# Attention and SoLU feed-forward on one core: u turned by block DMAs and VectorE's block transposes instead of by TensorE

## Chip, cores, metric

One core of one Trainium2 chip, all data in float32 (the two weights arrive as 64-bit floats and are taken apart by the kernel). The metric is the device time of one execution in microseconds (us), the median of several runs.

## The reference, cut to what matters

```python
# attention: batch 8, heads 8, 576 positions, head size 64
scores = scale * (q @ k^T)                       # 576 x 576 for each of 64 heads
scores = where(scores >= max - tau, scores, -1e9)
attn = exp(scores - max);  attn = attn / (sum + 1e-9)
x = (attn @ v)  -> (4608 tokens, 512)            # heads side by side

# feed-forward
h = x @ w_in                                     # 512 -> 1024
e = exp(h - max(h));  solu = h * e / (sum(e) + 1e-9)
ln = (solu - mean) / sqrt(var + 1e-6) * g_ln     # over the 1024
out = ln @ w_out                                 # 1024 -> 512
```

In the kernel `u` is h * e, before all scaling. A token tile has 128 tokens; there are 36.

## The kernel before

The kernel goes in 144 rounds. A round makes the scores of 128 query rows for two heads, and their threshold softmax; beside this, TensorE gets one more piece of work from a list: half of h, half of o (the product with w_out), or the attention with v of an earlier round. In the long middle four rounds repeat, and carry one token tile: h0, h1 (halves of h, with an attention each), o0, o1 (halves of o, of the tile before).

What each engine does, in the program's order (cut):

```python
# scores(s): s_ps, two tiles, ONE buffer each (4 PSUM banks)
nc.vector.tensor_reduce(out=nm, in_=ps[:, 0:S], axis=AX.X, op=ALU.max, negate=True)   # "maxima"
nc.scalar.activation(out=w, in_=ps[:, 0:S], func=AF.Prelu, bias=nth, ...)             # frees s_ps
nc.scalar.activation(out=w, in_=w, func=AF.Exp, ...)
nc.gpsimd.tensor_scalar(out=w, in0=w, scalar1=sm[:, x : x + 1], ...)                  # normalise
# blocks(s): 32x32 block transposes, then eight transfers put the blocks in place
nc.vector.transpose(out=T[:, :, r, h, :], in_=w)
nc.sync.dma_start(out=to[32 * a : ...], in_=T[...])           # wT <- T, x8 every second round
# attend: v times wT into a "pv" tile; next round ScalarE copies it out
nc.scalar.copy(out=to, in_=y)                                 # "attended", frees the pair of banks
```

PSUM is the memory that the matrix products are written to, in banks. `pv`, `h_ps` and `o_ps` share four more banks as two tiles of two banks (`take` hands out a free pair).

```python
def ff_exp(t):  nc.scalar.activation(out=d["u"], in_=d["h"], func=AF.Exp, ..., accum_out=d["se"])
def ff_mul(t):  nc.vector.tensor_tensor(out=d["u"], in0=d["h"], in1=d["u"], op=ALU.mult)

def u_item(t, f):                       # one half of u turned, rides on a round's scores
    def make(spare, x):
        for c in range(4):
            turn(spare, x + c, ...)     # 4 matmuls 64x64 with the identity into spare s_ps columns
    def keep(spare, x, r):
        (nc.vector.tensor_copy if r else nc.scalar.copy)(out=d["uT"][...], in_=seen(spare, r, x, 4))

def ff_o(t, part, split):               # one half of o: 32 matmuls 64x64 by 256
    for c in range(NC):
        for r in range(2):
            z = part ^ r                # row half r writes bank z; the banks change over at half time
            for y in range(2):
                mm = nc.tensor.matmul(out=o[ROWS[y], 512 * z : 512 * z + 256],
                    lhsT=d["uT"][ROWS[r], c, ROWS[y]], rhs=w2[ROWS[r], c, 256 * z : 256 * z + 256], ...)
                if part and not last: sync(mm, d["fence"])
# w2 is w_out * g_ln, centred over its rows, so that the mean needs no subtraction;
# ff_out: ob = o * rs  (rs = 1/sqrt(...) per token)
```

Of the kernel before, what the change touches and what calls it, by code (L numbers as in the profile page):

```python
# [20 lines left out]
def kernel(  # L21
# [43 lines left out]
    small = ctx.enter_context(tc.tile_pool(name="small", bufs=6))  # L65
# [4 lines left out]
    w2 = const.tile([P, NC, DM], F32, name="w2")  # L70
# [110 lines left out]

    def piece(x):
        if x < 2 * NP:
            c, hf = divmod(x, 2)
            cols = slice(512 * hf, 512 * hf + 512)
            return w_in[P * c : P * c + P, cols], w1[:, c, cols], W_UNIT
        c = x - 2 * NP
        return w_out[P * c : P * c + P, :], w2[:, c], gs[:, c : c + 1]
# [4 lines left out]
    def weight_load(x):  # L193
# [3 lines left out]
        (nc.scalar if x < 3 else nc.sync).dma_start(out=raw, in_=piece(x)[0])  # L197
        raws[x] = dict(raw=raw)

    def weight_a(x):  # L200
        if not wide:
# [4 lines left out]
            work.tile([P, 512], I32, tag=t, bufs=n, name="em") for t, n in (("em", 2), ("m", 1))  # L206
# [39 lines left out]
    totals = []  # L246

    def add_up(c):
        if c == 1:
            totals.append(work.tile([P, DM], F32, tag="ob", name="total"))  # L250
        if c:
            total = totals[0]
            nc.vector.tensor_tensor(
                out=total, in0=total if c > 1 else w2[:, 0], in1=w2[:, c], op=ALU.add
            )

    def mean():
        total = totals[0]
        ones = work.tile([P, P], F32, tag="ob", name="ones")
        nc.gpsimd.memset(ones, 1.0 / DFF)  # L260
        tag, m = take("mean")
        nc.tensor.matmul(out=m[:, 0:DM], lhsT=ones, rhs=total, start=True, stop=True)
        nc.scalar.copy(out=total, in_=m[:, 0:DM])
        pairs_free.append(tag)

    def center():
        for c in range(NC):
            nc.vector.tensor_tensor(out=w2[:, c], in0=w2[:, c], in1=totals[0], op=ALU.subtract)  # L268
# [162 lines left out]
    def ramp(s, x):  # L431
# [6 lines left out]
        w = work.tile([P, S], F32, tag="w", bufs=5, name="w")  # L438
# [24 lines left out]
    def blocks(s):  # L463
# [13 lines left out]
        u["wT"] = wT = work.tile([P, 2, NK, 2, 2, 32], F32, tag="wT", bufs=3, name="wT")  # L477
# [37 lines left out]
    def attended(key):  # L515
# [3 lines left out]
        if kind == 2:  # L519
            if b % 2 == 0:  # L520
                xe[b // 2] = work.tile([P, NP, P], F32, tag="xe", name="xe")
# [68 lines left out]
    def ff_stats(t):  # L590
# [18 lines left out]
        d["rs"] = rs  # L609


    def u_item(t, f):
        d = ffn[t]
        if f == 0:
            d["uT"] = work.tile([P, NC, P], F32, tag="uT", bufs=1, name="uT")
        d["turned"] = f + 1

        def make(spare, x):
            for c in range(4):
                o = P * (4 * f + c)  # L620
                turn(spare, x + c, lambda r, y: d["u"][ROWS[r], o + 64 * y : o + 64 * y + 64])

        def keep(spare, x, r):
            (nc.vector.tensor_copy if r else nc.scalar.copy)(
                out=d["uT"][:, 4 * f : 4 * f + 4, ROWS[r]], in_=seen(spare, r, x, 4)
            )

        return 4, make, keep


    def ff_t(t, f):
        d = ffn[t]
        if f == 0:
            d["uT"] = work.tile([P, NC, P], F32, tag="uT", bufs=1, name="uT")
        tp = ps_mm.tile([P, 1024], F32, tag="s1", name="tp_u")
        for c in range(4):
            o = P * (4 * f + c)
            nc.tensor.transpose(  # L638
                out=tp[:, P * c : P * c + P], in_=d["u"][:, o : o + P], identity=ident
            )  # L640
        (nc.vector.tensor_copy if f else nc.scalar.copy)(  # L641
            out=d["uT"][:, 4 * f : 4 * f + 4],
# [4 lines left out]
    def ff_o(t, part, split):  # L647
# [27 lines left out]
        if part == 0:  # L675
            d["fence"] = fence(last[-4:])
# [227 lines left out]
```

## Time and profile before

| | time | TensorE busy | VectorE | ScalarE | GpSimd |
|---|---|---|---|---|---|
| before | 963.9 us (962.7 to 966.0) | 93% | 66% | 68% | 49% |

The prediction below shows the lines. How to read them: a group has the source line, the engine, out<-in, the count, busy us, mean ns of one, and the idle time of that engine ahead of it with what ended it. In the windows view the columns are the stretch, its length, then busy us of TensorE (PE), its weight loads (PEld), VectorE (DVE), ScalarE (ACT), GpSimd (POOL), then the granted clock of TensorE, the DMA engines' share, and GB/s.

### The profile page before, as it was taken

Reading aid. Unit: us, or ns where it says so; the run is one execution under the profiler, and the core shown is the slowest. Engines: PE = TensorE matmul, PEld = TensorE weight load, DVE = VectorE, ACT = ScalarE, POOL = GpSimd, SP = SyncE. Lnnn points to the kernel's source line nnn. Section 1 sums busy time; section 2 is a strip of 40 time slices with the busy share of each in tenths; the row PEclk is TensorE's granted clock in tenths of the full one; section 3 lists DMA queues with packets and bytes.
Section 4 is the critical chain, followed back from the end, with each engine's and each line's share of the span. In section 5 each row is a group of like instructions: output and inputs, shape, how many; then the busy total and the mean of one; then the engine's idle time right before and its main releaser. Section 6 shows DMA issues by size and latency. Waiting matters only on the chain. (4 is left out here: it accounts for less than half of the span.)

```text
span 965.3 us, 43052 instructions
## 1 busy us (share of the span) xinstructions
PE 894.9 (93%) x18583; PEld 646.9 (67%) x18583; DVE 639.9 (66%) x1013; ACT 652.1 (68%) x1560; POOL 473.7 (49%) x898
## 2 busy tenths in 40 slices
PE   4657679999999999999999999999999999999997
PEld 3444446777767787777877776777867778665543
DVE  4889876667766667666666666666666666676221
ACT  5857656777867777777777776777777777776111
POOL 2886753555444545445454544445444555554111
PEclk9969798999999999999999999999999999999999
DMA  9897744875678447874678456864668445744200
GB/s 234 203 235 207 163 111 115 206 163 128 169 157 199 113 112 175 210 161 109 168 160 198 114 122 154 207 160 111 171 151 210 107 115 124 166 116 112 61 22 22
DMA packets 87037, 143.31 MB, mean 148 GB/s; under 512 B 28984, under 2 KB 61760, under 8 KB 86848
## 3 DMA queue, kind: packets, MB, share of 16 engines
q1 hardware_dynamic: 85616, 138.60, 60.4%
q8 instruction: 146, 2.39, 1.1%
q10 hardware_dynamic: 1232, 1.97, 0.7%
q14 instruction: 43, 0.35, 0.1%
HBM read 46.14 MB, written 9.44 MB: 58 GB/s over the span
## 5 line engine op out<-in xcount | busy, mean ns | idle before, releaser
L424 DVE TENSOR_REDUCE nm<-s_ps 128x1 f32<-128x576 f32 x288 | 204.7, 752 | 224.5 <-PE s_ps L408 224.4
L667 PE MATMUL o_ps<-w,uT 64*64 64x256 f32 x3968 | 233.7, 379 | 1.1 <-DVE w L268 1.1
L667 PEld LDWEIGHTS o_ps<-w,uT 64*64 64x64 f32 x3968 | 195.4, 134 | 51.9 <-issue 16.3
L439 ACT ACTIVATE w<-s_ps,nth 128x576 f32<-128x576 f32 x288 | 213.5, 741 | 22.2 <-issue 0.4
L459 POOL TENSOR_SCALAR w<-w,sm 128x576 f32<-128x576 f32 x288 | 215.4, 761 | 14.4
L449 ACT ACTIVATE w<-w,ntau 128x576 f32<-128x576 f32 x288 | 219.1, 764 | 0.0
L471 DVE STREAM_TRANSPOSE T<-w 128x576 f32<-128x576 f32 x288 | 207.8, 757 | 13.6 <-POOL w L459 6.6
L562 PE MATMUL h_ps<-w,xh 64*64 64x512 f32 x1856 | 214.7, 590 | 0.0
L435 ACT ACTIVATE nth<-nm,tau_t 128x1 f32<-128x1 f32 x288 | 85.9, 298 | 170.3 <-DVE nm L424 170.2
L510 PEld LDWEIGHTS pv<-wT,v 64*64 64x64 f32 x5760 | 166.0, 137 | 43.8 <-issue 39.4
L408 PE MATMUL s_ps<-kT,qT 64*64 64x512 f32 (+1 forms) x2048 | 171.9, 428 | 17.3 <-ACT w L439 12.4
L510 PE MATMUL pv<-wT,v 64*64 64x128 f32 (+1 forms) x5760 | 167.8, 264 | 12.2 <-DMA wT<-T 7.8
L456 POOL TENSOR_SCALAR sm<-sm 128x2 f32<-128x2 f32 x144 | 37.3, 259 | 277.8 <-ACT w L449 274.3
L562 PEld LDWEIGHTS h_ps<-w,xh 64*64 64x64 f32 x1856 | 107.5, 133 | 93.0 <-issue 88.0
L457 POOL TENSOR_TENSOR sm<-sm,mone 128x2 f32<-128x2 f32 x144 | 103.1, 716 | 12.0
L408 PEld LDWEIGHTS s_ps<-kT,qT 64*64 64x64 f32 x2048 | 57.3, 141 | 25.6 <-ACT w L439 19.0
L575 DVE TENSOR_REDUCE hm<-h_ps 128x1 f32<-128x1024 f32 x36 | 44.0, 1223 | 29.8 <-PE h_ps L553 18.0
L581 ACT ACTIVATE u<-h_ps,hm 128x1024 f32<-128x1024 f32 x36 | 40.1, 1114 | 28.4 <-DVE hm L575 27.7
L281 PE MATMUL s_ps<-ident,u 64*64 64x64 f32 x2016 | 50.0, 222 | 5.8 <-ACT w L439 2.4
L281 PEld LDWEIGHTS s_ps<-ident,u 64*64 64x64 f32 x2016 | 46.9, 135 | 12.3 <-ACT w L439 4.3
L449 ACT ACTIVATION_READ_ACCUMULATOR w<-w,ntau 128x1 f32 x288 | 54.7, 190 | 0.0
L104 POOL MEMSET mark<- 128x1 f32 x63 | 6.3, 99 | 95.8 <-PE o_ps L667 91.3
(89 smaller groups left out, 769.1 us busy)
## 6 DMA issues: line engine op xcount, KB each, us to landing
wT<-T SPq DMA_DIRECT2D x576, 144.0 KB, 3.2
v<-in_v_dram SPq DMA_DIRECT2D x64, 256.0 KB, 5.8
out_dram<-ob SPq DMA_DIRECT2D x32, 256.0 KB, 3.7
q<-in_q_dram SPq DMA_DIRECT2D x15, 512.0 KB, 5.7
k<-in_k_dram SPq DMA_DIRECT2D x15, 512.0 KB, 6.8
raw<-in_moe_w_out_dram SPq DMA_DIRECT2D x8, 512.0 KB, 5.4
raw<-in_moe_w_in_dram SPq DMA_DIRECT2D x5, 512.0 KB, 6.2
v<-in_v_dram SPq DMA_DIRECT2D x32, 64.0 KB, 5.5
```

Of the source, the lines that this page charges most:

```text
L281: nc.tensor.matmul(out=spare[r][ROWS[y], to], lhsT=lhsT_of(r, y), rhs=ident[ROWS[r], ROWS[r]], start=True, stop=True,)
L408: nc.tensor.matmul(out=ps[h][ROWS[y], ks], lhsT=lhsT, rhs=d["kT"][ROWS[h], ks], start=True, stop=True,)
L424: nc.vector.tensor_reduce(out=nm, in_=ps[:, 0:S], axis=AX.X, op=ALU.max, negate=True)
L435: nc.scalar.activation(out=nth, in_=d["nth"][x], func=AF.Identity, bias=tau_t, scale=1.0)
L439: nc.scalar.activation(out=w, in_=ps[:, 0:S], func=AF.Prelu, bias=nth, scale=1.0, alpha=1.0e30,)
L449: nc.scalar.activation(out=w, in_=w, func=AF.Exp, bias=ntau, scale=1.0, accum_out=sm[:, x : x + 1])
L457: nc.gpsimd.tensor_tensor(out=sm, in0=sm, in1=mone, op=ALU.pow)
L459: nc.gpsimd.tensor_scalar(out=w, in0=w, scalar1=sm[:, x : x + 1], scalar2=1.0, op0=ALU.mult, op1=ALU.mult)
L471: nc.vector.transpose(out=T[:, :, r, h, :], in_=w)
L510: nc.tensor.matmul(out=to, lhsT=d["v"][ROWS[u], h0 + h, m], rhs=rhs, start=m == 0, stop=m == NK - 1,)
L562: mm = nc.tensor.matmul(out=h[ROWS[y], f], lhsT=x[ROWS[r], c, ROWS[y]], rhs=w1[ROWS[r], c, f], start=part == 0 and c == 0, stop=part == 1 ...
L667: mm = nc.tensor.matmul(out=o[ROWS[y], 512 * z : 512 * z + 256], lhsT=d["uT"][ROWS[r], c, ROWS[y]], rhs=w2[ROWS[r], c, 256 * z : 256 * z + ...
```

## The change

The intent: take the turning of u (64 small matmuls with the identity per tile, and their evacuation) off TensorE, the engine that bounds the kernel. VectorE can transpose 32x32 blocks; to make a whole turn of those, eight transfers first move blocks of u across partitions into `V`. So that a row half of TensorE holds all features of its own tokens, w_out is kept twice (second copy with the row halves exchanged), and each row half adds up into one PSUM bank: no change of banks, no fence. u is normalised by ScalarE before it is moved, so w_out is not centred. For room, w has 4 buffers and not 5, wT 2 and not 3, small 3 and not 6, xe 1.

```diff
-    def u_item(t, f): ...                       # TensorE's turn, with its copies
+    def ff_norm(t):
+        nc.scalar.activation(out=d["u"], in_=d["u"], func=AF.Identity, bias=nb, scale=rs)
+    def ff_swap(t):
+        for r in range(2):
+            for g in range(2):
+                for y in range(2):
+                    to, of = 64 * r + 32 * g, 64 * r + 32 * y
+                    nc.sync.dma_start(out=V[to : to + 32, y],
+                        in_=d["u"][of : of + 32, DFF // 2 * g : DFF // 2 * g + DFF // 2])
+    def ff_turn(t, rnd):
+        nc.vector.transpose(out=uT, in_=d["V"].rearrange("p y (m x) -> p m y x", x=32))
     def ff_o(t, part):
+        for m in range(NC * part, NC * part + NC):
+            for r in range(2):
+                for z in range(2):
+                    nc.tensor.matmul(out=d["o"][ROWS[z], 512 * r : 512 * r + 256],
+                        lhsT=d["uT"][ROWS[r], m]..., rhs=w2[ROWS[r], m ^ r, 256 * z : 256 * z + 256], ...)
+    def weight_d(x):                            # the second copy of w_out
+        for r in range(2):
+            nc.sync.dma_start(out=w2[ROWS[r], 2 * c + 1], in_=w2[ROWS[1 - r], 2 * c])
-    add_up, mean, center                        # w_out's centring
 # schedule, rnd = the round h1 of the tile
-                middle.setdefault(rnd + 3, []).append(lambda t=cur: ff_stats(t))
+                middle.setdefault(rnd + 2, []).append(lambda t=cur: ff_stats(t))
+                late.setdefault(rnd + 2, []).append(lambda t=cur: (ff_norm(t), ff_swap(t)))
+                late.setdefault(rnd + 3, []).append(lambda t=cur, at=rnd + 3: ff_turn(t, at))
-                if busy and quarter < 2 and preps and ...: room = 0
+                if busy and quarter > 1 and preps and ...: room = 0
```

(Cut: w_out's loads in four 32-partition pieces, the order of g_ln, the output in two transfers, the buffers.)

More of the change, by code (lines that the diff above doesn't have):

```diff
@@ L64 @@
     work = ctx.enter_context(tc.tile_pool(name="work", bufs=2))
-    small = ctx.enter_context(tc.tile_pool(name="small", bufs=6))
+    small = ctx.enter_context(tc.tile_pool(name="small", bufs=3))
     ps_mm = ctx.enter_context(tc.tile_pool(name="ps_mm", bufs=1, space=PSUM))
@@ L69 @@
     w1 = const.tile([P, NP, DFF], F32, name="w1")
-    w2 = const.tile([P, NC, DM], F32, name="w2")
+    w2 = const.tile([P, 2 * NC, DM], F32, name="w2")
     mhalf = const.tile([P, 1], F32, name="mhalf")
@@ L179, in gains @@
         pairs_free.append(tag)
+    w_rows = w_out.rearrange("(g c r x) n -> c r g x n", g=2, r=2, x=32)
     def piece(x):
@@ L187, in piece @@
         c = x - 2 * NP
-        return w_out[P * c : P * c + P, :], w2[:, c], gs[:, c : c + 1]
+        return w_rows[c], w2[:, 2 * c], gs[:, c : c + 1]
     NW = 2 * NP + NC
@@ L196, in weight_load @@
         )
-        (nc.scalar if x < 3 else nc.sync).dma_start(out=raw, in_=piece(x)[0])
+        queue = nc.scalar if x < 3 else nc.sync
+        if x < 2 * NP:
+            queue.dma_start(out=raw, in_=piece(x)[0])
+        else:
+            for r in range(2):
+                for g in range(2):
+                    o = 64 * r + 32 * g
+                    queue.dma_start(out=raw[o : o + 32], in_=piece(x)[0][r, g])
         raws[x] = dict(raw=raw)
@@ L205, in weight_a @@
         d["em"] = e, m = [
-            work.tile([P, 512], I32, tag=t, bufs=n, name="em") for t, n in (("em", 2), ("m", 1))
+            work.tile([P, 512], I32, tag=t, bufs=n, name="em") for t, n in (("ob", 2), ("xe", 1))
         ]
@@ L243, in weight_c @@
         nc.gpsimd.tensor_tensor(out=dst, in0=dst, in1=d["em"][0].bitcast(F32), op=ALU.mult)
-    totals = []
-    def add_up(c):
-        if c == 1:
-            totals.append(work.tile([P, DM], F32, tag="ob", name="total"))
-        if c:
-            total = totals[0]
-            nc.vector.tensor_tensor(
-                out=total, in0=total if c > 1 else w2[:, 0], in1=w2[:, c], op=ALU.add
-            )
-    def mean():
-        total = totals[0]
-        ones = work.tile([P, P], F32, tag="ob", name="ones")
-        nc.gpsimd.memset(ones, 1.0 / DFF)
-        tag, m = take("mean")
-        nc.tensor.matmul(out=m[:, 0:DM], lhsT=ones, rhs=total, start=True, stop=True)
-        nc.scalar.copy(out=total, in_=m[:, 0:DM])
-        pairs_free.append(tag)
-    def center():
-        for c in range(NC):
-            nc.vector.tensor_tensor(out=w2[:, c], in0=w2[:, c], in1=totals[0], op=ALU.subtract)
+    def weight_d(x):
+        c = x - 2 * NP
+        if c >= 0:
+            for r in range(2):
+                nc.sync.dma_start(out=w2[ROWS[r], 2 * c + 1], in_=w2[ROWS[1 - r], 2 * c])
     SPARE = 7
@@ L437, in ramp @@
         )
-        w = work.tile([P, S], F32, tag="w", bufs=5, name="w")
+        w = work.tile([P, S], F32, tag="w", bufs=4, name="w")
         nc.scalar.activation(
@@ L476, in blocks @@
         T = T.rearrange("p (c m) r h x -> p c (m r h x)", c=2)
-        u["wT"] = wT = work.tile([P, 2, NK, 2, 2, 32], F32, tag="wT", bufs=3, name="wT")
+        u["wT"] = wT = work.tile([P, 2, NK, 2, 2, 32], F32, tag="wT", bufs=2, name="wT")
         to = wT.rearrange("p g m r h x -> p g (m r h x)")
@@ L520, in attended @@
             if b % 2 == 0:
-                xe[b // 2] = work.tile([P, NP, P], F32, tag="xe", name="xe")
+                xe[b // 2] = work.tile([P, NP, P], F32, tag="xe", bufs=1, name="xe")
             to = xe[b // 2][:, :, 64 * (b % 2) : 64 * (b % 2) + 64].rearrange(
@@ L608, in ff_stats @@
         nc.gpsimd.tensor_tensor(out=rs, in0=rs, in1=se, op=ALU.mult)
-        d["rs"] = rs
-    def u_item(t, f):
-        d = ffn[t]
-        if f == 0:
-            d["uT"] = work.tile([P, NC, P], F32, tag="uT", bufs=1, name="uT")
-        d["turned"] = f + 1
-        def make(spare, x):
-            for c in range(4):
-                o = P * (4 * f + c)
-                turn(spare, x + c, lambda r, y: d["u"][ROWS[r], o + 64 * y : o + 64 * y + 64])
-        def keep(spare, x, r):
-            (nc.vector.tensor_copy if r else nc.scalar.copy)(
-                out=d["uT"][:, 4 * f : 4 * f + 4, ROWS[r]], in_=seen(spare, r, x, 4)
-            )
-        return 4, make, keep
@@ L631, in ff_t @@
-    def ff_t(t, f):
-        d = ffn[t]
-        if f == 0:
-            d["uT"] = work.tile([P, NC, P], F32, tag="uT", bufs=1, name="uT")
-        tp = ps_mm.tile([P, 1024], F32, tag="s1", name="tp_u")
-        for c in range(4):
-            o = P * (4 * f + c)
-            nc.tensor.transpose(
-                out=tp[:, P * c : P * c + P], in_=d["u"][:, o : o + P], identity=ident
-            )
-        (nc.vector.tensor_copy if f else nc.scalar.copy)(
-            out=d["uT"][:, 4 * f : 4 * f + 4],
-            in_=tp[:, 0:512].rearrange("p (c q) -> p c q", c=4),
-        )
-        d["turned"] = f + 1
@@ L647, in ff_o @@
-    def ff_o(t, part, split):
+        nb = small.tile([P, 1], F32, tag="nb", name="nb")
+        nc.gpsimd.tensor_scalar(
+            out=nb, in0=mv[:, 0:1], scalar1=rs, scalar2=-1.0, op0=ALU.mult, op1=ALU.mult
+        )
+        d["norm"] = rs, nb
+    def ff_norm(t):
+        d = ffn[t]
+        rs, nb = d["norm"]
+        nc.scalar.activation(out=d["u"], in_=d["u"], func=AF.Identity, bias=nb, scale=rs)
+    def ff_swap(t):
+        d = ffn[t]
+        d["V"] = V = work.tile([P, 2, DFF // 2], F32, tag="V", bufs=1, name="V")
+        for r in range(2):
+            for g in range(2):
+                for y in range(2):
+                    to, of = 64 * r + 32 * g, 64 * r + 32 * y
+                    nc.sync.dma_start(
+                        out=V[to : to + 32, y],
+                        in_=d["u"][of : of + 32, DFF // 2 * g : DFF // 2 * g + DFF // 2],
+                    )
@@ L648, in ff_o @@
+    def ff_turn(t, rnd):
+        d = ffn[t]
+        d["uT"] = uT = work.tile([P, 2 * NC, 2, 32], F32, tag="uT", bufs=1, name="uT")
+        nc.vector.transpose(
+            out=uT, in_=d["V"].rearrange("p y (m x) -> p m y x", x=32)
+        )
+        d["turned"] = rnd + 1
+    def ff_o(t, part):
         d = ffn[t]
         if part == 0:
-            d["osplit"] = split
-            if split:
-                d["otag"], d["o"] = take("o_ps")
-            else:
-                d["o"] = ps_mm.tile([P, 1024], F32, tag="s0", name="o_ps")
@@ L655, in ff_o @@
-        o = d["o"]
-        if not d["osplit"]:
-            for c in range(4 * part, 4 * part + 4):
-                nc.tensor.matmul(
-                    out=o[:, 0:DM], lhsT=d["uT"][:, c], rhs=w2[:, c], start=c == 0, stop=c == NC - 1
-                )
-            return
-        last = []
-        for c in range(NC):
-            for r in range(2):
-                z = part ^ r
-                for y in range(2):
-                    mm = nc.tensor.matmul(
-                        out=o[ROWS[y], 512 * z : 512 * z + 256], lhsT=d["uT"][ROWS[r], c, ROWS[y]],
-                        rhs=w2[ROWS[r], c, 256 * z : 256 * z + 256],
-                        start=part == 0 and c == 0, stop=part == 1 and c == NC - 1,
-                    )
-                    if part and not last:
-                        sync(mm, d["fence"])
-                    last.append(mm)
@@ L675, in ff_o @@
-        if part == 0:
-            d["fence"] = fence(last[-4:])
+            d["otag"], d["o"] = take("o_ps")
+        for m in range(NC * part, NC * part + NC):
+            for r in range(2):
+                for z in range(2):
+                    nc.tensor.matmul(
+                        out=d["o"][ROWS[z], 512 * r : 512 * r + 256],
+                        lhsT=d["uT"][ROWS[r], m].rearrange("p y x -> p (y x)"),
+                        rhs=w2[ROWS[r], m ^ r, 256 * z : 256 * z + 256],
+                        start=m == 0, stop=m == 2 * NC - 1,
+                    )
@@ L680, in ff_out @@
         ob = work.tile([P, DM], F32, tag="ob", name="ob")
-        if d["osplit"]:
-            nc.scalar.activation(
-                out=ob.rearrange("p (z n) -> p z n", z=2),
-                in_=d["o"].rearrange("p (z n) -> p z n", z=2)[:, :, 0:256], func=AF.Copy,
-                scale=d["rs"],
-            )
-            pairs_free.append(d["otag"])
-        else:
-            nc.scalar.activation(out=ob, in_=d["o"][:, 0:DM], func=AF.Copy, scale=d["rs"])
         if len(t) == 1:
-            for x in range(2):
-                r = (2 * t[0] + x) * S + SM
-                nc.sync.dma_start(out=out[r : r + ST, :], in_=ob[ST * x : ST * x + ST])
+            rows = out.rearrange("(b s) m -> s b m", s=S)[SM:S, 2 * t[0] : 2 * t[0] + 2]
         else:
@@ L696, in ff_out @@
             rows = out[b * S : b * S + SM, :].rearrange("(p t) m -> t p m", t=4)
-            nc.sync.dma_start(out=rows[2 * kind + m], in_=ob)
+            rows = rows[2 * kind + m].rearrange("(r k) m -> k r m", r=2)
+        nc.scalar.copy(
+            out=ob.rearrange("p (r n) -> p r n", r=2),
+            in_=d["o"].rearrange("p (r n) -> p r n", r=2)[:, :, 0:256],
+        )
+        pairs_free.append(d["otag"])
+        for z in range(2):
+            nc.sync.dma_start(
+                out=rows[:, :, 256 * z : 256 * z + 256],
+                in_=ob[ROWS[z]].rearrange("p (r n) -> p r n", r=2),
+            )
     NS = len(slots)
@@ L741 @@
         load_v(0, 0)
-        nc.sync.dma_start(out=g_rows, in_=g_ln.rearrange("(c p) -> c p", p=P))
+        nc.sync.dma_start(
+            out=g_rows.rearrange("c (r g x) -> c r g x", r=2, g=2),
+            in_=g_ln.rearrange("(g c r x) -> c r g x", g=2, r=2, x=32),
+        )
         whole_pair(0)
@@ L754 @@
         quarter = 0
-        u_due = []
         w2_done = False
@@ L777 @@
                 room = SPARE
-                if u_due and u_due[0][0] <= rnd:
-                    _, t, f = u_due.pop(0)
-                    items.append(u_item(t, f))
-                    room -= 4
-                if busy and quarter < 2 and preps and rnd + 4 < first_slot(preps[0][3]):
+                if busy and quarter > 1 and preps and rnd + 4 < first_slot(preps[0][3]):
                     room = 0
@@ L794 @@
                 exps(rnd)
-            elif u_due and u_due[0][0] <= rnd:
-                for _, t, f in u_due:
-                    ff_t(t, f)
-                u_due = []
             if rnd in whole:
@@ L804 @@
                 weight_c(pieces[rnd - 1])
-            if pieces.get(rnd - 3) == 2 * NP + NC - 1:
-                mean()
             for job in middle.pop(rnd, []):
@@ L815 @@
             elif quarter == 2 or (prev is not None and not due):
-                if prev is None or (ffn[prev].get("turned") == 2 and w2_done):
+                if prev is None or (ffn[prev].get("turned", NS + rnd) <= rnd and w2_done):
                     step = ("o", 0)
@@ L829 @@
                 late.setdefault(rnd + 1, []).append(lambda t=cur: ff_mul(t))
-                middle.setdefault(rnd + 3, []).append(lambda t=cur: ff_stats(t))
+                middle.setdefault(rnd + 2, []).append(lambda t=cur: ff_stats(t))
+                late.setdefault(rnd + 2, []).append(lambda t=cur: (ff_norm(t), ff_swap(t)))
+                late.setdefault(rnd + 3, []).append(lambda t=cur, at=rnd + 3: ff_turn(t, at))
             elif step == ("o", 0):
                 if prev is not None:
-                    ff_o(prev, 0, rnd + 1 < NS)
+                    ff_o(prev, 0)
                 quarter = 3
@@ L836 @@
                 if prev is not None:
-                    ff_o(prev, 1, None)
+                    ff_o(prev, 1)
                     begin.setdefault(rnd + 1, []).append(lambda t=prev: ff_out(t))
-                if cur is not None:
-                    u_due += [(rnd + 1, cur, 0), (rnd + 2, cur, 1)]
                 prev, cur = cur, None
@@ L863 @@
                     weight_a(x + 1)
-            x = pieces.get(rnd - 2, -1) - 2 * NP
-            if x > 0:
-                add_up(x)
-            if pieces.get(rnd - 3) == 2 * NP + NC - 1:
-                center()
-                w2_done = True
+            if rnd - 2 in pieces:
+                weight_d(pieces[rnd - 2])
+                w2_done = pieces[rnd - 2] == NW - 1
             rnd += 1
```

## The prediction

> **What bounds the kernel now.** I read the page first, for busy shares and slices, then the windows by stage, then the timelines of TensorE, VectorE, ScalarE and the DMA queue around 340 to 360 us, then the timeline of the end.
>
> ```profile
> PE 894.9 (93%) x18583; PEld 646.9 (67%) x18583; DVE 639.9 (66%) x1013; ACT 652.1 (68%) x1560; POOL 473.7 (49%) x898
> PE   4657679999999999999999999999999999999997
> ...
> 164.50:891.00 726.50, 718.05 (x16114) 543.28 (x16107) 498.19 (x796) 534.28 (x1283) 362.99 (x727) 1.00 0.64 152
> 0.00:164.50 164.50, 110.88 (x2095) 71.49 (x2099) 122.92 (x194) 107.02 (x258) 102.28 (x147) 0.87 0.75 184
> 891.00:966.00 75.00, 65.99 (x381) 32.11 (x379) 18.80 (x25) 10.80 (x19) 8.39 (x24) 0.98 0.12 34
> ```
>
> From 164 to 891 us TensorE is busy 99% at the full clock, and nothing else is over 74%. So the long middle is TensorE's order of work; the start (weights, DMA) and the end (feed-forward of the last tiles) are stages of their own. The middle repeats every four rounds of scores: h first half, h second half, o first half, o second half (called h0, h1, o0, o1 here), one token tile a cycle. From the times at which ScalarE starts each round, the cycle is 23.9 us on average (round 20 at 150.5 us, round 142 at 879.1: 728.6 / 122 x 4).
>
> ```profile
> 353.21 3.72 PE L667 MATMUL o_ps<-w,uT 64*64 64x256 f32 x64
> 356.67 0.71 PE L281 MATMUL s_ps<-ident,u 64*64 64x64 f32 x30
> ...
> 355.27 1.51 DVE L471 STREAM_TRANSPOSE T<-w 128x576 f32<-128x576 f32 x2
> 358.36 1.42 DVE L424 TENSOR_REDUCE nm<-s_ps 128x1 f32<-128x576 f32 x2 [1.58 <-PE s_ps L408]
> ...
> 356.84 5.44 SPq L482 DMA_DIRECT2D wT<-T  x8
> ...
> wT<-T SPq DMA_DIRECT2D x576, 144.0 KB, 3.2
> SPq L482 <- DVE T L471: 318.0, 69, 9.5
> ```
>
> To see: one of the two transposes of u costs TensorE 0.5 us (356.67 until the scores start at 357.17). VectorE waits 1.6 us for scores, so it has slack, but only that. Eight transfers of one group keep the DMA queue for 5.4 us, 0.64 us from issue to issue; each lands 3.2 us after its issue (2.3 at the least). The queue spends 318 us waiting at its head for VectorE's T.
>
> **What the Trainium skill says.** "DMA: Bandwidth & Descriptors", section Rules for kernel authors: many small transfers should be made into a large one; below 64 KB one pays mostly overhead. The new ones have just 64 KB. The trace agrees in kind: 0.5 KB of tau took 4.3 us to land, 144 KB took 3.2. Same page, Anatomy of one DMA: DMA engines do not wait on semaphores; any wait is on the issuing sequencer before dispatch. The 318 us above are such waits, so whatever stands behind one in the queue waits too. "Perfetto Trace Analysis", Per-instruction lifecycle, on DMA: the reported time ends when the sequencer is free, the data movement comes after; hence 0.59 us in the timeline and 3.2 to land. "VectorE: DVE Perf Modes", The three transpose paths: VectorE transposes only 32x32 blocks; that is why DMAs must first move blocks across partitions.
>
> **The change, part by part.**
>
> Off TensorE: 36 tiles less the 4 or 5 of the end, two u-transposes each, 63 x 0.5 to 0.55 us = 33 us. The fences of o are worth under 3 us (TensorE's weight loads waited 2.6 us for the mark). The matrix products of o stay 64 per tile of 64x64 by 256, in four quadrants as before; I take 3.46 us a half as now (348.03 to 351.49). The preparations of q and k move from the o to the h rounds: no cost in sum.
>
> Off the evacuation: 63 copies on each of VectorE (414 ns) and ScalarE (364 ns). On: ScalarE one 128x1024 pass (as the exponential, 1.11 us), VectorE one 128x1024 transpose. T's 576 columns take 0.72 us, so 1024 take about 1.2. GpSimd one more small operation, 0.34. In sum ScalarE +17 us, VectorE +17 us: neither binds by its sum.
>
> On the DMA queue: eight 64 KB transfers a tile, 8 x 0.64 = 5.1 us, and one more output transfer. Two wT groups 10.9, V 5.1, outputs 1.3, loads (18 a batch of 4.5 tiles) 2.6: 20 of 23.9 us. It fits in sum. But the order counts. In the built program V's transfers stand directly behind a wT group, that of round o1; and the VectorE transpose of V stands in h0 of the next cycle, just **before the maxima of h1**. VectorE works in order, so late V means late maxima.
>
> The chain, from the start of ScalarE's work in o1 (time 0, TensorE then begins its o half):
> - VectorE: second maximum to 0.67, statistics 1.52 to 2.2, blocks 1.44 to 3.65 (statistics now stand before the blocks).
> - GpSimd: normalises the former round to about 1.4, two operations 0.9, five 2.0: 4.4. ScalarE's new pass ends at 5.6. So the pass is not what V waits for.
> - Queue: wT issued 3.7 to 8.8, V 8.8 to 13.9; the last V issue starts at 13.3 and lands 2.3 to 3.2 later, 15.6 to 16.5.
> - VectorE transposes V to 16.8 (17.7). Without it the maxima of h1 could start at 11.5 (TensorE: o half to 2.7, scores and preparation 4.4, h half 7.9, attention 9.9, preparation and scores 11.5). They start 5 to 6 us late.
> - First maximum 0.75: ScalarE starts h1 at 17.6. From the timeline, with preparations: both halves of the scores free after 2.3, exponentials to 3.9, exponential of h and the copy of the attention to 5.5, so ScalarE starts o0 at 23.1. TensorE has run scores of o0 from 20.0 and its o half to 24.5.
> - ScalarE lets the scores' banks go at 25.2; the scores of o1 and the maximum take 2.05: **o1 starts again at 27.3**, 28.2 with the later landing. The loop is closed, and 27.3 > 23.9.
>
> In the stretches where q, k and v are loaded (1 or 2 tiles of 4.5) their issues stand before wT, and wT transfers land in 5 to 6 us (368.43 to 373.76): 1 to 2 us more. Mean cycle some 28 us: +4.1 x 30.5 cycles = **+125 us** (an estimate; +104 if every landing is the shortest).
>
> The end: before, a tile takes 15.7 us there (maxima at 929.11 and 944.80). Now from a tile's maximum: 3.9 to the product, statistics 1.5, GpSimd 2.1, pass 1.2, V 5.1 + 2.3, transpose 1.2 = 17.3 before the next maximum on VectorE. +1.6 x 3 = 5. The last tile's o started 8.6 after its maximum (944.80 to 953.43), now 17.3: +9. Together +14.
>
> The start: VectorE loses 10.6 us (sums 4.8, centring 5.8), the queue gets 16 copies of w_out x 0.64 = 10 us and 24 more load issues, and two V groups. I set 0, with 10 either way.
>
> Sum: 964 + 125 + 14 = 1103; with the shortest landings 1082. I take 1090, as small gaps may be filled by what I counted in series.
>
> **The rivals.**
> 1. V lands in time and TensorE stays the bound. For: VectorE and ScalarE are 66% busy, V has a whole round between issue and use, the attention's buffers still cover their three rounds. Then 964 - 33 - 3 + 14 = 942, with some gain at the start 935. Against: 16 issues at 0.64 us are measured, and the transpose's place in VectorE's order is fixed. For this to be so, V would have to land 5 us sooner.
> 2. The wait is there but half hidden, as blocks of the h1 round find more slack or V's issues are faster for 2 KB rows: a cycle of 25 to 26 us, some 1000 to 1040.
> 3. Fewer buffers bind (wT 3 to 2, w 5 to 4, small 6 to 3). In the order, w of a round is transposed before the maxima of the next but one, and a wT buffer is free one round before its refill; so nothing, unless V delays attention. It would add to the loss, to 1130.
>
> **Range and chances.** The order and the issue time are certain, the landing and the loads less. 1040 to 1130 covers the main case with an error of a third of the +125 downward. Rival 1 gets about 0.08, most of it just over 2% faster; the narrow band within 2% 0.05; slower 0.87.
>
> **What would show it.** Right: VectorE's uT transpose, 36 times, idle before it for 5 us or more each (150 us and over in sum), ended by DMA V<-u; eight V transfers in a block behind eight wT; TensorE busy down to 8 tenths in the middle, its scores waiting for ScalarE's w; cycle 27 to 29 us; the end 14 us longer. Wrong: uT's transpose with no idle time, TensorE at 99% in the middle and a cycle of 22.8 us; or V landing within 10 us of o1's start. If TensorE's o half is not 3.46 us, my assumption on the two banks is wrong.

## More of the kernel before

One fact that I had on the page and did not use is the row of granted clock:

```profile
PEclk9969798999999999999999999999999999999999
```

One digit is a fortieth of the span, 9 is 90% or more of full speed. It is below 9 only at the start, where TensorE waits.

## The result, and the profile after

| | time | ratio to before | TensorE busy | granted clock |
|---|---|---|---|---|
| before | 963.9 us (4 runs) | 1 | 93% | 0.98 |
| changed | 1205.6 us (1202.0 to 1209.1, 4 runs) | 1.2505 (1.246 to 1.255) | 80% | 0.875 |

The clocks are means over the profiled runs.

A quarter slower: the direction that was foretold, and twice its size. The page of the changed kernel, busy and granted clock in 40 slices, then the groups of the new transpose and of o:

```profile
PE   4567677788988788888888888888888888888785
...
PEclk8878788999888888888888888888888888888898
...
L642 PE MATMUL o_ps<-w,uT 64*64 64x256 f32 x4608 | 322.5, 439 | 44.1 <-ACT xh L524 27.5
...
L630 DVE STREAM_TRANSPOSE uT<-V 128x1024 f32<-128x1024 f32 x36 | 44.8, 1245 | 315.3 <-DMA V<-u 304.4
```

The transpose itself is cheap, 1.245 us each; VectorE stands idle 315 us ahead of its 36 instances, and for 304 of these the transfers into V were the last to come. That was the predicted sign. Two things were not predicted: one instruction of o lasts 439 ns where it lasted 379, and the clock is down through the whole middle.

One cycle in the timelines (start, length, engine, line, out<-in, count, idle before). The round o1 starts on ScalarE at 441.50. In the changed kernel L417 are the maxima, L464 the blocks, L475 the transfers wT, L401 the scores, L642 o, L524 the copy of the attention.

```profile
447.70 1.50 DVE L464 STREAM_TRANSPOSE T<-w 128x576 f32<-128x576 f32 x2 [1.07 <-POOL w L452]
458.52 1.25 DVE L630 STREAM_TRANSPOSE uT<-V 128x1024 f32<-128x1024 f32 x1 [9.32 <-DMA V<-u]
459.69 1.38 DVE L417 TENSOR_REDUCE nm<-s_ps 128x1 f32<-128x576 f32 x2
...
444.93 4.96 SPq L475 DMA_DIRECT2D wT<-T  x8
449.99 6.87 SPq L622 DMA_DIRECT2D V<-u  x8
```

The eight V transfers stand behind the eight of wT; VectorE waits 9.3 us for the last of them, with the maxima of h1 behind the transpose. Then ScalarE and TensorE:

```profile
460.44 0.29 ACT L428 ACTIVATE nth<-nm,tau_t 128x1 f32<-128x1 f32 x1 [9.31 <-DVE nm L417]
...
464.52 1.09 ACT L574 ACTIVATE u<-h_ps,hm 128x1024 f32<-128x1024 f32 x1
465.52 0.19 ACT L574 ACTIVATION_READ_ACCUMULATOR u<-h_ps,hm 128x1 f32 x1
465.61 0.36 ACT L524 COPY xh<-pv 128x256 f32<-128x256 f32 x1
...
462.15 0.48 PE L401 MATMUL s_ps<-kT,qT 64*64 64x64 f32 x4 [4.00 <-ACT qe L348]
463.16 2.19 PE L401 MATMUL s_ps<-kT,qT 64*64 64x64 f32 x12 [0.53 <-ACT w L432]
466.02 6.66 PE L642 MATMUL o_ps<-w,uT 64*64 64x256 f32 x64 [0.68 <-ACT xh L524]
```

TensorE is idle for 4.0 us, makes the scores slowly, then waits for ScalarE's copy of the attention, which frees the bank pair that o0 takes; and the o half lasts 6.5 us (466.02 to the next scores at 472.51) where the next one, o1, and those of before last 3.5. The windows view of the same stretch says why:

```profile
452.00:456.00 4.00, 4.00 (x48) 2.74 (x42) 0.00 (x0) 0.00 (x0) 1.48 (x2) 1.00 0.43 104
456.00:460.00 4.00, 2.16 (x63) 1.88 (x59) 1.48 (x2) 0.00 (x0) 0.00 (x0) 1.00 0.45 104
460.00:464.00 4.00, 1.32 (x12) 0.80 (x16) 4.00 (x8) 3.39 (x10) 0.00 (x0) 0.73 1.05 219
464.00:468.00 4.00, 3.33 (x28) 1.26 (x24) 2.79 (x5) 3.76 (x9) 2.41 (x4) 0.50 1.12 213
468.00:472.00 4.00, 4.00 (x41) 2.25 (x40) 1.21 (x2) 1.68 (x5) 2.05 (x4) 0.50 1.03 222
472.00:476.00 4.00, 4.00 (x76) 2.43 (x72) 2.30 (x4) 1.34 (x4) 1.16 (x3) 0.99 0.65 202
```

The third column from the right is the clock: after the idle time it is granted at 0.5 for about ten microseconds. Over the middle of this run (rounds 20 to 142) the half clock holds for 219 us, in stretches of 3.4, 6.8 or 10.2 us, in nearly every cycle; before, it held for 3 us there.

One long gap is not needed for it. The clock changes on a grid of 3.41 us. In the middle of the changed kernel 29 stretches of half clock begin; in the 3.41 us ahead of each, TensorE was busy for 0 to 49%, and in 12 of the 29 no single gap reached 3.4 us. From 267.3 to 270.7 us, for instance, the gaps were 0.7 and 1.7 us, TensorE was busy for 1.31 us, and the half clock began. Of the 182 such steps after which the full clock stayed, the least busy one had 42%.

Where the time went by stage, from the starts of ScalarE's rounds in the two profiled runs: up to round 20, 150.5 to 157.2 us (+6.7); rounds 20 to 142, 728.6 to 942.5 (+213.9); the rest 86.2 to 102.9 (+16.7). The middle is 30.5 cycles, so 23.9 to 30.9 us a cycle.

### The profile page after: what moved, and what is told of

It is laid out like the page before. It is cut to its first block, busy times and chain, and to the rows that moved or that the text cites. A ratio compares the mean times of both kernels' runs of the same rounds, so it can differ in the third digit from the quotient of the medians.

```text
span 1202.6 us, 40518 instructions
## 1 busy us (share of the span) xinstructions
PE 959.6 (80%) x17089; PEld 574.6 (48%) x17089; DVE 640.6 (53%) x963; ACT 663.0 (55%) x1531; POOL 478.8 (40%) x902
## 5 line engine op out<-in xcount | busy, mean ns | idle before, releaser
L642 PE MATMUL o_ps<-w,uT 64*64 64x256 f32 x4608 | 322.5, 439 | 44.1 <-ACT xh L524 27.5
L417 DVE TENSOR_REDUCE nm<-s_ps 128x1 f32<-128x576 f32 x288 | 203.5, 747 | 181.3 <-PE s_ps L401 178.7
L642 PEld LDWEIGHTS o_ps<-w,uT 64*64 64x64 f32 x4608 | 202.3, 158 | 203.6 <-issue 73.0
L401 PE MATMUL s_ps<-kT,qT 64*64 64x64 f32 (+1 forms) x2048 | 197.5, 477 | 125.3 <-ACT w L432 52.8
L464 DVE STREAM_TRANSPOSE T<-w 128x576 f32<-128x576 f32 x288 | 208.5, 758 | 22.8 <-POOL w L452 22.5
L630 DVE STREAM_TRANSPOSE uT<-V 128x1024 f32<-128x1024 f32 x36 | 44.8, 1245 | 315.3 <-DMA V<-u 304.4
L503 PEld LDWEIGHTS pv<-wT,v 64*64 64x64 f32 x5760 | 159.5, 137 | 55.5 <-issue 38.7
L503 PE MATMUL pv<-wT,v 64*64 64x128 f32 (+1 forms) x5760 | 166.1, 265 | 14.7 <-DMA wT<-T 11.6
L555 PEld LDWEIGHTS h_ps<-w,xh 64*64 64x64 f32 x1856 | 84.9, 135 | 118.9 <-issue 104.3
L401 PEld LDWEIGHTS s_ps<-kT,qT 64*64 64x64 f32 x2048 | 61.8, 150 | 149.0 <-ACT w L432 66.5
L611 ACT ACTIVATE u<-u,nb,rs 128x1024 f32<-128x1024 f32 x36 | 44.7, 1240 | 43.9 <-POOL nb L603 43.9
L590 DVE BATCH_NORM_STATS2 bs<-u 128x6 f32<-128x512 f32 x72 | 46.0, 680 | 0.1
```

What stands on the lines that cost most here:

```text
L401: nc.tensor.matmul(out=ps[h][ROWS[y], ks], lhsT=lhsT, rhs=d["kT"][ROWS[h], ks], start=True, stop=True,)
L503: nc.tensor.matmul(out=to, lhsT=d["v"][ROWS[u], h0 + h, m], rhs=rhs, start=m == 0, stop=m == NK - 1,)
L555: mm = nc.tensor.matmul(out=h[ROWS[y], f], lhsT=x[ROWS[r], c, ROWS[y]], rhs=w1[ROWS[r], c, f], start=part == 0 and c == 0, stop=part == 1 ...
L590: nc.vector.bn_stats(out=bs[:, f], in_=u[:, 512 * f : 512 * f + 512])
L642: nc.tensor.matmul(out=d["o"][ROWS[z], 512 * r : 512 * r + 256], lhsT=d["uT"][ROWS[r], m].rearrange("p y x -> p (y x)"), rhs=w2[ROWS[r], m ...
```

## The experiments

The theory after the result: V lands late, because it stands behind wT in one queue; VectorE waits for it ahead of the maxima; so ScalarE, the scores and TensorE come late; and TensorE's idle time costs more than itself, since o0 then runs at half clock and waits for a bank. The rivals: the mere load of the new work, wherever it waits; and the fewer buffers. Twelve kernels ran, and all are told. Unless it is said, they give the right result.

### Turn one round later

```diff
# e1_turn_late, on the changed kernel
-                late.setdefault(rnd + 3, []).append(lambda t=cur, at=rnd + 3: ff_turn(t, at))
+                last.setdefault(rnd + 4, []).append(lambda t=cur, at=rnd + 4: ff_turn(t, at))
             for job in late.pop(rnd, []): job()
+            for job in last.pop(rnd, []): job()
```

> The changed kernel, but VectorE's transpose of V stands one round later: behind the maximum of the next tile's h in round h1, no longer ahead of the maxima of h1. Theory (late V stops VectorE, which stops ScalarE, the scores and so TensorE, whose clock then falls): V has 5 us more and nothing of the attention stands behind it, so VectorE's idle time before this transpose falls from 315 us to under 60, the half clock goes from the middle, the cycle falls from 30.9 to 23 to 25 us, and the time to 940 to 1000 us. Rival 1 (the eight transfers and the new pass cost time by their load on the queue and the engines, wherever the transpose stands): over 1100. Rival 2 (fewer buffers of w, wT and small): over 1100.

Measured: 1012.6 us, ratio 1.048 (1.041 to 1.055). VectorE's wait, from the list of who waited for whom (us in total, times, longest):

```profile
DVE uT L630 <- DMA V<-u: 56.1, 25, 9.9
```

One instruction moved on VectorE takes back 193 of the 242 us. The load and the buffers are as in the changed kernel, so neither rival can be the main cause. It is a little above the range that I wrote, and does not reach before.

### The wait alone taken away

```diff
# e2_no_wait, on the changed kernel: wrong result on purpose
-            out=uT, in_=d["V"].rearrange("p y (m x) -> p m y x", x=32)
+            out=uT, in_=d["u"].rearrange("p (y m x) -> p m y x", y=2, x=32)
```

> The changed kernel, but VectorE transposes u itself in place of V; V's transfers are still issued and land, and nothing reads them. The result is wrong on purpose. Theory: only the wait is taken away, all load stays; the cycle is what TensorE's work gives, 22.5 to 24 us, TensorE 97% busy in the middle at full clock, and 930 to 965 us in all. Rival 1 (load on the queue): still over 1100, as the queue has the same 8 transfers a tile.

Measured: 994.6 us, ratio 1.030 (1.026 to 1.035). So the wait for V, with all that follows from it, is 211 of the 242 us (1205.6 - 994.6). But I missed here: 930 to 965 was expected. 30 us above before remain, and the gain on TensorE is not to be seen either. Two waits that were not in the changed kernel's list of large ones:

```profile
ACT u L574 <- DMA V<-u: 23.5, 13, 6.0
...
PE pv L503 <- DMA wT<-T: 20.0, 11, 5.6
```

The next tile's exponential must not overwrite u before the transfers have read it, and the attention waits for wT. Both are the queue's.

### No transfers at all

```diff
# e6_no_transfers, on e2_no_wait: wrong result on purpose
     def ff_swap(t):
         d = ffn[t]
+        return
```

> As e2_no_wait (VectorE transposes u itself, wrong on purpose), and V's transfers are not issued at all. It asks for the 29 us that e2_no_wait is still above before, and for the 33 us that TensorE should save. Theory A (eight more issues a tile delay the attention's transfers and the next product on u, in the stretches with loads): 930 to 955 us, cycle 22.5 to 24 us everywhere. Theory B (ScalarE's new pass behind GpSimd, or the order of the o rounds): 980 to 1000 us as e2_no_wait.

Measured: 928.8 us, ratio 0.960 (0.954 to 0.966): theory A, a little below its range. The windows view of this kernel (middle, start, end):

```profile
141.00:845.00 704.00, 690.38 (x14383) 445.00 (x14374) 508.94 (x766) 544.11 (x1258) 366.24 (x723) 1.00 0.68 158
0.00:141.00 141.00, 92.04 (x1675) 64.01 (x1679) 105.70 (x163) 99.34 (x237) 92.80 (x136) 0.81 0.89 210
845.00:929.00 84.00, 75.42 (x1048) 44.26 (x1040) 29.01 (x37) 21.37 (x37) 17.99 (x45) 0.98 0.20 49
```

TensorE is 98% busy in the middle at full clock, the cycle is 23.1 us (703.4 / 30.5; before 23.9). So the arithmetic of the change, the pass and the transpose included, is worth 35 us: by the profiled runs 25 in the middle (728.6 to 703.4), 9 at the start and 1 at the end. The transfers that make it right cost 66 us by being in the queue (994.6 - 928.8) and 211 us by being waited for.

### Issues or bytes

```diff
# e10_small_transfers, on e2_no_wait: wrong result on purpose
-                        out=V[to : to + 32, y],
-                        in_=d["u"][of : of + 32, DFF // 2 * g : DFF // 2 * g + DFF // 2],
+                        out=V[to : to + 32, y, 0:64],
+                        in_=d["u"][of : of + 32, DFF // 2 * g : DFF // 2 * g + 64],
```

> As e2_no_wait (nobody reads V, wrong on purpose), with V's eight transfers a tile an eighth as long: 8 KB each in place of 64 KB. e2_no_wait took 994.6 us and e6_no_transfers, without them, 928.8. If the number of issues on the queue is what costs: 980 to 1000 us. If it is the bytes on the DMA engines: 928 to 945. In between: both.

Measured: 988.1 us, ratio 1.021 (1.013 to 1.029). An eighth of the bytes saves 6 of the 66 us; the other 59 stay. So it is not the 512 KB a tile that cost. I take it to be the eight places in the queue, 5 us of it a tile; but the packets are as many in both runs (107,662), so a cost of each packet is not told apart from that of an issue. (This run was on another chip than e2_no_wait's; the ratios, each to runs of before on its own chip, say the same.) To make four transfers of the eight is not tested on the chip.

### The clock by itself

```diff
# e3_warm, on the changed kernel
                 attend(attending)
+                if step == ("h", 1) and rnd > 18:
+                    warm(attending)      # 40 matmuls 64x64 by 256 into unused columns of pv's banks
```

> The changed kernel, with 40 matrix products of no use (64x64 by 256, some 4.3 us at full clock) behind the attention in every h1 round, into unused columns of its bank, where TensorE now waits for scores. The result stays right. If the half clock that follows the wait is a cost of its own: the o half of o0 falls from over 5 us back to 3.5, the middle stays at full clock, the cycle falls by 1.5 to 3 us, and the time to 1110 to 1160 us although TensorE has more to do. If the clock costs nothing beyond the wait (the wait sets the cycle alone): 1195 us or more.

Measured: 1178.5 us, ratio 1.219 (1.214 to 1.225): outside the range, though TensorE does 136 us of work more and the kernel is 27 us faster. The half clock in the middle falls from 219 to 58 us, and the o half of o0 from 5.4 to 4.0 us (mean of 25 cycles, first to last instruction; before 3.35). So the clock has a cost of its own. It is smaller than I wrote because o0 starts no sooner, 24.2 us after o1's start and 23.9 in the changed kernel: its half is quick again, but waits for the copy of the attention.

```profile
528.31 3.68 PE L655 MATMUL o_ps<-w,uT 64*64 64x256 f32 x64 [1.67 <-ACT xh L537]
```

### The bank that o0 waits for

```diff
# e7_warm_copy_first, on e3_warm
-                begin.setdefault(rnd + 1, []).append(lambda key=attending: attended(key))
+                if step == ("h", 1):
+                    late[rnd].insert(0, lambda key=attending: attended(key))   # before ff_exp
+                else:
+                    begin.setdefault(rnd + 1, []).append(lambda key=attending: attended(key))
```

> As e3_warm, and in h1 rounds ScalarE copies the attention out of its bank before the exponential of h, no longer after it. Theory: o0 cannot start before that copy frees its bank pair, so with the clock kept the copy sets the cycle: o0 starts 1.0 to 1.3 us sooner, the cycle falls by as much, 1135 to 1155 us against e3_warm's 1178. If the bank is not what o0 waits for: 1170 to 1185.

Measured: 1131.5 us, ratio 1.171 (1.1645 to 1.1765), 47 us less than e3_warm and a little below the range. o0 starts at 22.9 (24.2), its half lasts 3.5 us (4.0), and the mean cycle falls from 30.4 to 28.6 us. So of the 1.8 us a cycle, 1.2 are the earlier start; the rest is half clock that e3_warm still had (58 us in the middle, here 29). The copy first without the extra products was not run. TensorE's timeline in one cycle (the 80 are the extra products):

```profile
529.67 4.50 PE L513 MATMUL pv<-w 64*64 64x256 f32 x80
533.99 1.43 PE L401 MATMUL s_ps<-kT,qT 64*64 64x64 f32 x16
535.99 3.68 PE L655 MATMUL o_ps<-w,uT 64*64 64x256 f32 x64 [0.57 <-ACT xh L537]
```

With both effects nearly taken away the cycle is 28.6 us, still with VectorE waiting for V in every cycle (305 us in all). That is close to the chain of the prediction by itself, which gave 27.3 to 28.2, some 28 with the loads.

### V ahead of wT in the queue

```diff
# e12_swap_first, on the changed kernel
-                middle.setdefault(rnd + 2, []).append(lambda t=cur: ff_stats(t))
-                late.setdefault(rnd + 2, []).append(lambda t=cur: (ff_norm(t), ff_swap(t)))
+                middle.setdefault(rnd + 2, []).append(
+                    lambda t=cur: (ff_stats(t), ff_norm(t), ff_swap(t)))      # before blocks
```

> The changed kernel, but in each o1 round V's eight transfers stand ahead of the attention's eight in the queue, no longer behind them. Theory (the place in the queue makes V late): V's first issue comes when ScalarE's pass is done, 5.6 us after o1's start and not 8.9, and V lands by 13 to 14 us and not 16.4, the cycle falls by 3 us or more and the half clock with it, 1070 to 1130 us; not all the way, as the attention's transfers are now 7 us later and TensorE will wait for them in h1. If V's lateness does not matter: 1190 to 1215.

Measured: 1178.7 us, ratio 1.221 (1.213 to 1.229). The first half of the expectation held: V's first issue comes 6.2 us after o1's start and not 8.9, the last lands at 13.5 and not 16.4, ScalarE starts h1 at 15.9 and not 18.5. The time did not follow: it lies far above the range, and the half clock still holds for 193 us in the middle. The list of waits:

```profile
DVE uT L630 <- DMA V<-u: 197.7, 34, 10.2
PE pv L503 <- DMA wT<-T: 135.7, 57, 5.9
```

The attention's wait for wT, 11.6 us in the changed kernel, is now 136: one wait took the place of the other. Both groups are urgent at that point, and the queue needs 5 us for either.

### Another queue for V, or for the loads

```diff
# e8_late_pool_v, on e1_turn_late: V's transfers issued by GpSimd
-                    nc.sync.dma_start(out=V[to : to + 32, y], ...
+                    nc.gpsimd.dma_start(out=V[to : to + 32, y], ...
# e9_late_pool_loads, on e1_turn_late: loads of q, k, v (from the second batch on) issued by GpSimd
-    nc.sync.dma_start(...)
+    (nc.gpsimd if b else nc.sync).dma_start(...)
```

> As e1_turn_late, and V's transfers are issued by GpSimd instead of the SyncE queue. It asks whether their place behind the attention's transfers is what is left. If so: V lands some 3 us sooner, the SyncE queue has its old load back, 940 to 985 us, a version that could beat before. If GpSimd's issuing holds back its own normalising: 1010 us or more.

> As e1_turn_late, and the loads of q, k and v from the second batch on are issued by GpSimd instead of SyncE. If the stretches with loads lose because 18 issues a batch stand before the attention's and V's transfers in one queue: cycles of 27 to 30 us there fall to 24 to 25, 950 to 990 us. If it is the load on the DMA engines themselves: 1000 to 1020 as e1_turn_late.

Measured: 1046.6 us, ratio 1.083 (1.076 to 1.090), and 1039.1 us, ratio 1.075 (1.067 to 1.082): both slower than e1_turn_late; e9 fits neither of its two cases. For e8, the group of V's issues and the largest new wait:

```profile
L622 POOL DMA_DIRECT2D V<-u x288 | 145.5, 512 | 62.1 <-ACT u L611 53.2 <-ACT w L432 4.5 <-issue 2.8
```

```profile
DVE T L464 <- POOL w L452: 214.5, 39, 10.0
```

GpSimd works in order too: it waits for ScalarE's pass, spends 0.5 us on each issue, and the normalising of the softmax stands behind, for which VectorE's blocks then wait 215 us. What holds e9 back I did not settle: GpSimd spends 86 us on those issues, k lands in 9.2 us (6.8 in e1_turn_late), and no single wait explains the rest. V from ScalarE's queue was not tried.

### Turn late and copy first

```diff
# e11_late_copy_first: the edits of e1_turn_late and of e7_warm_copy_first's copy
```

> As e1_turn_late (1012.6 us), and in h1 rounds the attention's copy stands ahead of the exponential of h on ScalarE. If o0 still waits for the bank of that copy there: 0.5 to 1.3 us less a cycle, 975 to 1000 us. If with the turn late only the full queue is left: 1005 to 1020.

Measured: 1008.6 us, ratio 1.044 (1.038 to 1.051): the same as e1_turn_late within the intervals. With the turn late the bank is no longer what counts; the full queue is what is left. None of the versions with the right result beats before.

### The buffers

```diff
# e4_buffers, on the kernel before
-    small ... bufs=6        tag="w", bufs=5   tag="wT", bufs=3   tag="xe" (2)
+    small ... bufs=3        tag="w", bufs=4   tag="wT", bufs=2   tag="xe", bufs=1
```

> The kernel before, with the changed kernel's fewer buffers alone (small 3, w 4, wT 2, xe 1). Theory: nothing waits for them, 960 to 970 us, within 1% of before. Rival 2: slower by 2% or more, up to a large share of the 242 us.

Measured: 965.4 us, ratio 0.9996 (0.995 to 1.004). The buffers cost nothing, at least in the kernel before.

### One part alone: w_out not centred

```diff
# e13_not_centred, on the kernel before (small has 5 buffers)
-                middle.setdefault(rnd + 3, []).append(lambda t=cur: ff_stats(t))
+                middle.setdefault(rnd + 2, []).append(lambda t=cur: ff_stats(t))
+                late.setdefault(rnd + 2, []).append(lambda t=cur: ff_norm(t))
-    add_up, mean, center;  scale=d["rs"] of the output's copy
```

> The kernel before with one part of the change alone: w_out not centred, u normalised by ScalarE's pass, the output copied without a scale; TensorE still turns u (small has 5 buffers in place of 6, for room). e6_no_transfers reached round 20 9 us sooner than before. If that is the missing sums and centring: round 20 at 141 to 144 us and not 150.5; the middle unchanged (cycle 23.9) if ScalarE's pass fits beside; the end some 8 us longer, as the turning there waits for the statistics. In sum 955 to 968 us. If the pass holds ScalarE up in the middle: 980 or more.

Measured: 1131.4 us, ratio 1.170 (1.167 to 1.174). This missed by far, and was my own making. In the kernel before, TensorE turns u at the very start of h0, ahead of the scores; now it must wait there for ScalarE's pass:

```profile
467.32 3.72 PE L676 MATMUL o_ps<-w,uT 64*64 64x256 f32 x64
474.50 0.73 PE L281 MATMUL s_ps<-ident,u 64*64 64x64 f32 x30 [3.46 <-ACT u L618]
```

So an idle time of 3.5 us in a cycle, in TensorE's order of work, again with a fallen clock (0.914 over the run), and a cycle of 28.9 us in place of 23.9. It says nothing clean of the centring: round 20 is reached at 146 us, 4 us sooner than before, where e6_no_transfers was 9 sooner; how much of those 9 is the centring stays open. But it is a second, independent case of a wait of 3 to 4 us in each cycle making the cycle 5 us longer.

## Why the prediction was wrong

The direction and the wait for V were right. The size was not: 1090, 1040 to 1130 foretold, 1205.6 measured; the chain behind the wait left two things out. By its own steps; times are us from ScalarE's start of o1, measured as means of 25 cycles (rounds 42 to 138) of the changed kernel's profiled run:

| step of the chain | predicted | measured |
|---|---|---|
| VectorE's blocks done | 3.65 | 3.4 |
| ScalarE's pass done | 5.6 | 5.5 |
| first, last V issue | 8.8, 13.3 | 8.9, 14.1 |
| last V landing | 15.6 to 16.5 | 16.4 |
| transpose of V done | 16.8 to 17.7 | 17.9 |
| ScalarE starts h1 | 17.6 | 18.5 |
| ScalarE starts o0 | 23.1 | 23.9 |
| TensorE's o half of o0, start | 21.0 | 23.9 |
| ... its length, to the next scores | 3.46 | 5.6 |
| o1 starts again | 27.3 to 28.2 | 31.4 |

1. **Right: the wait and its place.** V behind wT, VectorE's transpose ahead of the maxima, idle 304 us for V. Taking the wait away gives back 211 us (e2), moving the transpose 193 (e1).

2. **Wrong: the step from o0 to the next o1.** From ScalarE's start of o0 it took 4.2 us in the prediction (23.1 to 27.3) and 7.5 in the run (23.9 to 31.4). The prediction let TensorE run scores of o0 from 20.0 "and its o half to 24.5", that is, begin it at 21.0, at once and at full clock. Two things were left out. First, the o half needs a PSUM bank pair, and there are two; the one it takes is freed by ScalarE's copy of the attention, which the prediction itself put at the end of ScalarE's h1 round, 23.1. I used that time for ScalarE's next round and did not ask who waits for the copy. Second, the clock. The Trainium skill, "TensorE: Matmul & The Clock Gate", section HAM oscillation, warns of idle gaps over about 3.4 us between bursts, after which the clock falls to half. I did not look it up, since the page showed full clock in the middle. This trace agrees: after 4.0 us of idle time the clock is 0.50, and the half lasts 6.5 us in place of 3.5. But the runs are stricter than that: shorter gaps did it too, where TensorE was busy for less than about half of a 3.41 us step (see the profile after).

   Each was shown by an experiment: keeping the clock -27 us (e3), the copy first -47 more (e7, some of it the clock again), and then the cycle is 28.6 where the chain said some 28. In the middle the prediction had +125 us and the run +214; e3 and e7 together, 74 us, are most of those 89, and in e3 some half clock remained.

3. **Slightly short: the queue.** I counted 0.64 us an issue; that is the median, and leaves out the longer issues that are in many groups (the group of wT that the prediction shows took 5.4 us, 0.68 an issue). V's group took 6.9 us and not 5.1 in the cycle shown (two of its issues took 1.4 and 1.6 us; what held them the trace does not say for sure), and the last issue came 0.8 us late in the mean. "It fits in sum" was true of the average and hid that even unread the eight issues cost 59 to 66 us (e2, e6, e10).

4. **Near enough: the end and the start.** +14 foretold, +16.7 measured for the end, though a tile took 16.6 us there (1155.74 to 1172.38) and not 17.3, so the parts are less near than the sum; 0 with 10 either way, +6.7 for the start.

5. **Rivals.** Rival 1, V in time, gave 935 to 942; the kernel without transfers took 929. That is nearer than its parts: the middle gained 25 us where 33 to 36 were counted on TensorE, and the start 9. The saving is real, and the transfers ate it. Rival 3, the buffers, is refuted in the kernel before (e4). The middle way of rival 2 is what e1 shows when the transpose is moved.

## What to carry to other kernels

Where engines work in order, ask of each new wait not only how long it is but what stands behind it on that engine: the same transpose one round later took back 80% of the loss. When a wait will leave TensorE less than half busy for some 3.4 us in every cycle, count the half clock that followed here as part of its price, and follow every buffer that the late engine frees, PSUM banks above all. And count a DMA queue by its transfers and by who stands behind whom, not by bytes or by its mean load.

## What the Trainium skill lacked or had wrong

- "DMA: Bandwidth & Descriptors", Issuing engines are not separate DMA queues, calls the sequencer's time to initiate a DMA "usually small relative to the DMA itself", and the page gives no time in us for an issue from SyncE on this chip. Here an issue takes 0.63 us from one to the next in the median, for 8, 64 and 144 KB alike (e10, changed kernel); a 64 KB transfer between SBUF partitions lands in 2.0 us (changed kernel; 2.4 in e2) and an 8 KB one in 1.8 (e10). Eight transfers a tile cost 59 us of 964 with an eighth of the bytes, 66 with all.
- The same page has no time that an issue takes from GpSimd's own work: 0.51 us each, and 4.4 us from issue to landing where SyncE's took 2.1 (e8, e1).
- "TensorE: Matmul & The Clock Gate" speaks of idle gaps over about 3.4 us, and prices a matmul loop that pays for one in every turn. In these runs shorter gaps did it as well: in the middle of the changed kernel 12 of 29 stretches of half clock began without a gap of 3.4 us, and in e12 all 30; TensorE was busy for 0 to 49% of the 3.41 us before. What no page has is what it is worth to fill the gap when another wait stands behind it: idle products took the half clock from 219 to 58 us of the middle, and the kernel became only 27 us faster.
